# Planned attention and feed-forward kernel: first-pass sums held until a tile's last gate, gates ranked early, two kinds of copies moved to VectorE

## The chip, the cores and the metric

The kernel runs on one core of one Trainium2 chip. A core has five engines that run side by side, each with its own queue worked off in order: TensorE (PE, matrix products; its weight loads are shown as PEld), VectorE (DVE), ScalarE (ACT), GpSimd (POOL) and SyncE (SP, which only issues DMAs here). Data lies in DRAM, in SBUF (128 partitions) and in PSUM, which takes the products of TensorE and has eight banks of 128 x 512 float32. The metric is device time in microseconds: the median of several runs. Smaller is better.

## The reference

```
scores = 0.125 * q @ k.T            # 8 batches x 8 heads, 576 tokens, head size 64
scores = where(block_i >= block_j, scores, -1e9)      # blocks of 64 tokens
attn = softmax(scores) @ v
x = attn.transpose(0, 2, 1, 3).reshape(4608, 512)     # tokens x heads*size
h = x @ w_in                                          # 512 -> 2048
g = h * erf(softplus(h))
out = g @ w_out                                       # 2048 -> 512
```

Everything is float32. The kernel keeps float32 accuracy by splitting operands: each is written as a high part that TensorE takes exactly (fp32r, or fp16 for the probabilities) and a low part, the difference, and a product is made of three matmuls (high x high, high x low, low x high).

## The kernel before

**A plan.** The kernel does not issue its instructions as it builds them. Each step is put into a `Plan` with `add(engine, estimated ns, function, reads, writes)` and takes the priority `plan.prio` of that moment (a smaller number goes first). `Plan.order` then walks through estimated time, engine by engine: of the steps whose inputs are ready and whose buffers are free, the one with the smallest priority runs next. The order found there is the order in each engine's queue on the chip. `HOP` and `SPARE` are the extra time that it assumes between a step and one on another engine that needs it, the second for TensorE and for PSUM banks. Buffers of a tag in SBUF are given out in the order in which the steps were added; PSUM banks go to whoever asks first. A `token` is a buffer without memory that limits how many of something are under way.

**Attention** takes 64 heads, one for each `slot` n (0 to 63, with four more to run out). In slot n the plan adds: the load of head n+3 (`load_qk`: a DMA for `st` and one issued by GpSimd, two copies in SBUF by DMA, and the low parts on GpSimd, L456 and L457; four buffers `qks`); the maxima of head n+2 (`maxes`: scores `s` on TensorE L468, row maxima on VectorE L472 and L498, turned by TensorE and ScalarE and written by a small DMA `qk<-mt` into a row of q); the probabilities of head n (`probs`: scores `t`, L521 and L522; exp on ScalarE, L528, into `p32s`; the fp16 high part `ph` on ScalarE, L536, and the difference `pl` on VectorE, L537); for every second slot the products with v of a pair of heads (`pv`: `u`, L567, sums `us`, L593). Four heads are a quad; after each quad `normalise` makes reciprocals (L614), spreads them out (`rw`, L621, on ScalarE), turns them on TensorE (`rb`, L629), multiplies (`xs`, L632, VectorE), makes the high part (L634, ScalarE) and the low part (L635, GpSimd), and writes both to `x_d` in DRAM (L636). This is done once for each of the two pairs (`m(0)`, `m(1)`). The whole numbers of slots are the priorities; `PV` and the like shift some.

**First feed-forward pass.** Of 16 blocks of 128 hidden features the first `F1` = 6 are worked off for 18 tiles of `T` = 256 tokens, two blocks at a time: 3 `unit`s a tile, 54 in all. A unit (`moe_unit`) is: `up`, 24 matmuls into one PSUM bank `m_h` (L342); `gate`, a formula of one tanh (L314), four squares (L320) on ScalarE, two VectorE steps (L324, L328), then the high part `gh` (L329, ScalarE) and the low part `gl` (L330, GpSimd); `down`, 12 matmuls into two PSUM banks `o` (L363), one for each 128 tokens. A tile's `o` is summed over its three units; `store` copies it out (`ob`, L670) and writes it to `part_d`. A tile is known once its batch is normalised. The loop at the end of each slot adds units of known tiles:

```
at = max(n + BEHIND, 9 + BEHIND + (NT // T * NU - len(units1)) * spread)
if at - PACE > n and n < N + 3:
    break
unit1(at, False)
```

With `BEHIND` 1 and `PACE` 0, `at` is above n in every slot, so that units are added only in slot 67, with priority 68 or somewhat more and their gates at 65 (`GATE` -3). The last `TAIL` = 5 units have priorities of their own, from 70.

**Weights** are split by `load_weight` in two halves each: four or five VectorE steps (L287, L289, L292, L295, L297), two on ScalarE, two on GpSimd (L300, L301), with temporary buffers from the tags that gates and x use too. The six blocks of the first pass are added in the slots listed in `W1`, four of the second pass by `early_w2` after the last head, the others later.

**Second pass.** The other 10 blocks run over 9 tiles of 512 tokens; a unit is one block. The first tile also splits the weights that aren't there yet. At its end the sum of the first pass is added and written to the output. Some of its buffers (`w2`, `b`, `g`) exist only when all of attention is done.

Of the kernel before, what the change touches and what calls it, by code (L numbers as in the profile page):

```python
# [10 lines left out]
F16 = mybir.dt.float16  # L11
# [44 lines left out]
class Plan:  # L56
# [4 lines left out]
    SPARE = 500.0  # L61
    SWITCH = 90.0

# [4 lines left out]
    def add(self, eng, ns, fn, r=(), w=(), lag=0.0, mode="f", off=0.0):  # L68
        t = Task(len(self.tasks), eng, ns, lag, fn, self.prio + off, mode, self.era)
        for k in r:  # L70
            if k in self.written:
                t.deps.add(self.written[k])
            self.read.setdefault(k, []).append(t)
        for k in w:
            if k in self.written:
                t.deps.add(self.written[k])
            t.deps.update(self.read.pop(k, ()))
            self.written[k] = t
        t.deps.discard(t)
# [12 lines left out]
        self.tasks.append(t)  # L92
        return t
# [97 lines left out]
def tile_attention_moe(ctx: ExitStack, tc: tile.TileContext, qk, v, w, maskrows, sels, out):  # L191
# [21 lines left out]
    GATE = -3.0  # L213
# [90 lines left out]
    def gate(h, kh, n, name, gpool):  # L304
# [5 lines left out]
        bgh, bgl = (buf(gpool, [P, n], F32R, t, f"{name}_{t}") for t in ("gh", "gl"))  # L310
        br = [buf("m", [P, n], F32, t, f"{name}_{t}") for t in ("r0", "r1")]
        regs = [(br[0], br[0])]
        free = [((lambda: f32(bgl())), bgl), (br[1], br[1])]
        add("ACT", 690, lambda: nc.scalar.activation(br[0](), h(), AF.Tanh, bias=const(p1), scale=p0), r=kh, w=[br[0]])  # L314
        for k, (o, pp) in enumerate(zip(PROG, pars)):
            free += [regs[i] for i in sorted(set(o[1:])) if last[i] == k]
# [16 lines left out]
    def moe_unit(ws, xs, o, tw, nu, u, name, first, last, spread, oh, nh, gpool, at, rate, after=None):  # L333
# [19 lines left out]
        plan.prio = at + GATE  # L353
# [38 lines left out]
    p32s = [spool.tile([P, n], F32, name=f"p32_{i}") for i, n in enumerate(PN)]  # L392
    nc.gpsimd.memset(p32s[0][64:128, 768:], 0.0)
# [6 lines left out]
    ident16 = spool.tile([P, P], F16, name="id16")  # L400
    nc.vector.tensor_copy(ident16, ident)
# [108 lines left out]
    def probs(n, out):  # L510
# [4 lines left out]
        def one(j, q0, w_):  # L515
# [4 lines left out]
            def go():  # L520
# [7 lines left out]
            add("ACT", 160 + 0.84 * (w_ - skip), lambda: nc.scalar.activation(p32s[pt][:kk, c : c + w_ - skip], s()[:kk, skip:w_], AF.Exp, scale=SCALE),  # L528
                r=[s], w=[("p32", pt, j, q0)])

        def split(pt, keys):
            p = p32s[pt]
            ph = buf("a", [P, PN[pt]], F16, f"ph{pt}", f"ph{pt}_{n}", 4)
            pl = buf("a", [P, PN[pt]], F16, f"pl{pt}", f"pl{pt}_{n}", 4)
            keys = [("p32", pt, *k) for k in keys]
            add("ACT", 850, lambda: nc.scalar.copy(ph(), p), r=keys, w=[ph])  # L536
            add("DVE", 1250, lambda: nc.vector.tensor_tensor(out=pl(), in0=p, in1=ph(), op=ALU.subtract), r=keys + [ph], w=[pl])  # L537
            out.append((ph, pl))
# [62 lines left out]
    def normalise(b, qd, usbs, rs, krs):  # L601
# [14 lines left out]
        def m(pp):  # L616
            c = 2 * qd + pp
            xs = buf("a", [P, 2, S], F32R, "xs", f"xs_{nm}_{pp}")
            rw = buf("a", [P, 5, 2, D], F32, "rw", f"rw{nm}_{pp}", 1)
            for hf, k in enumerate((3, 2)):  # L620
                add("ACT", 510 - 110 * hf, lambda hf=hf, k=k: nc.scalar.copy(rw()[:, 3 * hf : 3 * hf + k], ri()[:, pp, :k, hf, :].unsqueeze(3).broadcast_to([P, k, 2, D])),  # L621
                    r=[ri], w=[(rw, hf)])
# [11 lines left out]
            add("ACT", 670, lambda: nc.scalar.copy(xs()[:, 0, :], f32(xs()[:, 1, :])), r=[(xs, 0), (xs, 1)], w=[(xs, 2)])  # L634
# [20 lines left out]
    os, hold = {}, {}  # L655
# [17 lines left out]
    def unit1(at, tail):  # L673
        t, u = units1.pop(0)
        plan.prio = at
        for s in (t, t + 1):
            if s in known and s not in x1:
                x1[s] = load_x("x", s * T, T)
        if u == 0:
# [3 lines left out]
                 hold[t], 3 if tail else NH, "g" if tail else "m", at, 0.05, marks.get(slot))  # L683
# [25 lines left out]
    def next_w1():  # L709
        plan.era = 0  # L710
        w1.append(room("w", len(w1)))
        load_weight(w1[-1], (("x", ("xh", "xl"), 2 * DM, 2), ("m", "r0", DM, 3), ("m", "r1", DM, 3)), len(w1) - 1)
# [11 lines left out]
    for slot in range(N + 4):  # L724
# [60 lines left out]
    def next_weight():  # L785
        if len(w2) < NF - F1:
            w2.append(room("w2" if len(w2) < NB + 2 else "w", F1 + len(w2)))
            load_weight(w2[-1], (("x", ("xh", "xl"), 2 * DM, 2), ("m", "gh", DM, 3), ("m", "gl", DM, 3)), F1 + len(w2) - 1)

    base = N + 6.0  # L790
# [88 lines left out]
```

## Time and profile before

| | us |
|---|---|
| median of 3 runs | 1395.18 |
| lowest, highest | 1393.9, 1398.31 |
| the profiled execution | 1394.03 |
| its span, first to last instruction | 1392.3 |

| engine | busy us | share of the span | instructions |
|---|---|---|---|
| TensorE | 1254.5 | 90% | 8168 |
| ScalarE | 973.5 | 70% | 1781 |
| VectorE | 804.2 | 58% | 1237 |
| GpSimd | 591.1 | 42% | 456 |

The profile comes from one execution, which has its own time. Busy times are shares of a span with stages of different limits, so the table alone doesn't say what bounds the kernel. The granted clock is the share of full speed that TensorE was given; its mean over the span is 0.922. In the views below an instruction is named by its source line (L320), its engine, and its output and input tiles; x576 is a count.

### The profile page before, as it was taken

How to read it: one execution, taken by the hardware profiler on the slowest of the kernel's cores; microseconds unless marked ns; L12 is line 12 of the kernel's file. 1: busy time of each engine (PE TensorE's matmuls, PEld its weight loads, DVE VectorE, ACT ScalarE, POOL GpSimd, SP SyncE). 2: the span in 40 equal slices, each digit the busy share in tenths (PEclk: the TensorE clock that was granted, in tenths of full speed). 3: DMA queues.
4: the chain of work that ended last, by engine and by line, in shares of the span. 5: the costliest groups of instructions: out<-in, count | busy, mean ns of one | idle time of the engine just before them, and what ended most of it. 6: DMA issues, size and time to landing. Idle time of an engine off the chain costs nothing.

```text
span 1392.3 us, 22070 instructions
## 1 busy us (share of the span) xinstructions
PE 1254.5 (90%) x8168; PEld 1038.4 (75%) x8168; DVE 804.2 (58%) x1237; ACT 973.5 (70%) x1781; POOL 591.1 (42%) x456
## 2 busy tenths in 40 slices
PE   7456688889998999999999998779999999999997
PEld 3345576677777778788989987568888888888885
DVE  4988867888777788886532218953333233333232
ACT  1445557788776787789877768557677676776764
POOL 5666545576564566654432225632222222222221
PEclk9756778899999999999999999889999999999999
DMA  9556376787767677753473223203203113113010
GB/s 238 150 139 161 94 201 170 185 209 204 190 181 176 169 199 207 179 158 124 154 255 105 91 76 137 76 2 120 99 23 122 61 61 121 61 61 121 1 61 31
DMA packets 89372, 179.97 MB, mean 129 GB/s; under 512 B 8540, under 2 KB 27292, under 8 KB 89264
## 3 DMA queue, kind: packets, MB, share of 16 engines
q1 hardware_dynamic: 79280, 159.41, 38.5%
q0 software_dynamic: 9344, 18.97, 6.5%
q8 instruction: 65, 1.06, 0.3%
q10 hardware_dynamic: 640, 0.17, 0.1%
q14 instruction: 43, 0.35, 0.1%
HBM read 112.29 MB, written 37.75 MB: 108 GB/s over the span
## 4 chain that ended last, share of the span: by engine, by line
PE 53%; DVE 5%; ACT 2%; issue 1%; DMA 1%; DVEq 0%; ACTq 0%
PE o L363 25%; PE m_h L342 24%; DVE bits L287 1%; DVE bits L289 1%; PE u L567 1%; DVE m_r L324 1%; DMA qk<-mt 1%; PE t L521 1%; ACT m_r L320 1%; PE t L522 1%; PE s L468 1%; DVE sq L292 0%; DVE pl L537 0%; DVE bits L295 0%; PE rt L611 0%
## 5 line engine op out<-in xcount | busy, mean ns | idle before, releaser
L320 ACT ACTIVATE m_r<-m_r,c 128x512 f32<-128x512 f32 x576 | 406.3, 720 | 88.1 <-DVE m_r L324 61.6
L330 POOL TENSOR_TENSOR m_gl<-m_r,m_gh 128x512 fp32r<-128x512 f32 x144 | 189.0, 1314 | 511.8 <-ACT m_gh L329 298.4
L324 DVE SCALAR_TENSOR_TENSOR m_r<-m_r,m_r 128x512 f32<-128x512 f32 x144 | 125.6, 873 | 289.7 <-ACT m_r L320 268.7
L342 PE MATMUL m_h<-xh,whi 128*128 128x256 f32 (+1 forms) x648 | 208.9, 322 | 0.1
L342 PE MATMUL m_h<-xl,whi 128*128 128x256 f32 (+1 forms) x648 | 207.4, 320 | 0.0
L342 PE MATMUL m_h<-xh,wlo 128*128 128x256 f32 (+1 forms) x648 | 207.3, 320 | 0.0
L472 DVE TENSOR_REDUCE mx<-s 64x1 f32<-64x288 f32 (+4 forms) x384 | 163.9, 464 | 61.2 <-PE s L468 60.5
L528 ACT ACTIVATE p<-t 128x288 f32<-128x288 f32 (+4 forms) x384 | 135.3, 386 | 74.1 <-PE t L522 32.6
L363 PE MATMUL o<-whi,m_gh 128*128 128x512 f32 x432 | 173.7, 402 | 14.6 <-ACT m_gh L329 14.3
L521 PE MATMUL t<-qk 69*128 69x288 f32 (+4 forms) x384 | 136.3, 359 | 45.0 <-DMA qk<-mt 15.5
L328 DVE SCALAR_TENSOR_TENSOR m_r<-m_r,m_h 128x512 f32<-128x512 f32 x144 | 98.7, 685 | 134.5 <-ACT m_r L320 134.5
L363 PE MATMUL o<-wlo,m_gh 128*128 128x512 f32 x432 | 172.6, 400 | 0.0
L537 DVE TENSOR_TENSOR pl<-p,ph 128x832 f16<-128x832 f32 (+1 forms) x128 | 151.6, 1186 | 28.9 <-ACT ph L536 28.6
L468 PE MATMUL s<-qk 68*128 68x256 f32 (+3 forms) x384 | 119.4, 372 | 42.6 <-DVE mx L472 24.9
L314 ACT ACTIVATE m_r<-m_h,c 128x512 f32<-128x512 f32 x144 | 98.5, 684 | 78.1 <-PE m_h L342 77.2
L456 POOL TENSOR_TENSOR qk<-st,qk 64x576 fp32r<-64x576 f32 x64 | 106.6, 1669 | 69.8 <-DMA qk<-qk 40.0
L457 POOL TENSOR_TENSOR qk<-st,qk 64x576 fp32r<-64x576 f32 x64 | 108.1, 1688 | 60.9 <-DMA qk<-qk 57.7
L342 PEld LDWEIGHTS m_h<-xh,whi 128*128 128x128 f32 x648 | 124.5, 192 | 10.9 <-DVE mx L472 0.4
L342 PEld LDWEIGHTS m_h<-xl,whi 128*128 128x128 f32 x648 | 124.5, 192 | 10.0
L342 PEld LDWEIGHTS m_h<-xh,wlo 128*128 128x128 f32 x648 | 124.3, 192 | 8.5
L522 PE MATMUL t<-qk 128*128 128x288 f32 (+4 forms) x384 | 126.2, 333 | 0.0
L363 PE MATMUL o<-whi,m_gl 128*128 128x512 f32 x432 | 126.1, 394 | 0.0
(83 smaller groups left out, 2357.9 us busy)
## 6 DMA issues: line engine op xcount, KB each, us to landing
st<-qk SPq DMA_DIRECT2D x64, 288.0 KB
qk<-qk POOLq DMA_DIRECT2D x64, 288.0 KB, 4.8
qk<-qk SPq DMA_DIRECT2D x64, 288.0 KB
x_d<-xs SPq DMA_DIRECT2D x32, 576.0 KB
raw<-w SPq DMA_DIRECT2D x32, 512.0 KB
v<-v SPq DMA_DIRECT2D x16, 640.0 KB
qk<-qk SPq DMA_DIRECT2D x64, 144.0 KB
xh<-x_d SPq DMA_DIRECT2D x18, 512.0 KB
```

The costliest lines, as they stand in the source:

```text
L320: add("ACT", 722, lambda r=r, a=a, pp=pp: nc.scalar.activation(r[0](), a[0](), AF.Square, bias=const(pp[1]), scale=pp[0]), r=[a[1]], w=[r[1]])
L324: add("DVE", 890, lambda r=r, a=a, c=c, pp=pp, ops=ops: nc.vector.scalar_tensor_tensor(out=r[0](), in0=a[0](), scalar=pp[0], in1=c[0](), o ...
L330: add("POOL", 1450, lambda: nc.gpsimd.tensor_tensor(out=bgl(), in0=g[0](), in1=f32(bgh()), op=ALU.subtract), r=[g[1], bgh], w=[bgl])
L342: nc.tensor.matmul(hk()[:, k, :], lhsT=a(0)[:, cc * P : (cc + 1) * P], rhs=x()[:, cc, :], start=cc == 0 and i == 0, stop=cc == NCC - 1 and ...
L363: nc.tensor.matmul(o[c](), lhsT=a()[:, sl], rhs=b_(1), start=first and k == 0 and not lo and b_ is whi, stop=last and k == nu - 1 and lo)
L457: add("POOL", 1780, lambda: nc.gpsimd.tensor_tensor(out=t[D:, 1, :], in0=st()[D:, :], in1=f32(t[D:, 1, :]), op=ALU.subtract), r=[st], w=Q( ...
L468: add("PE", mmns(w_), lambda: nc.tensor.matmul(s()[:r, c0 : c0 + w_], lhsT=qh[:K, i * P : i * P + r], rhs=kh[:K, k0 : k0 + w_], start=True ...
L472: add("DVE", 145 + 1.07 * w_, lambda: nc.vector.tensor_reduce(out=mx[:r, col : col + 1], in_=s()[:r, c0 : c0 + w_], axis=AX.X, op=ALU.max, ...
L521: nc.tensor.matmul(s()[:kk, :w_], lhsT=kh[:K, ks], rhs=qh[:K, q0 : q0 + w_], start=True, stop=False)
L522: nc.tensor.matmul(s()[:kk, :w_], lhsT=klh[:, ks], rhs=qhl[:, q0 : q0 + w_], start=False, stop=True)
L528: add("ACT", 160 + 0.84 * (w_ - skip), lambda: nc.scalar.activation(p32s[pt][:kk, c : c + w_ - skip], s()[:kk, skip:w_], AF.Exp, scale=SCALE),
L537: add("DVE", 1250, lambda: nc.vector.tensor_tensor(out=pl(), in0=p, in1=ph(), op=ALU.subtract), r=keys + [ph], w=[pl])
```

## The change

Times in the plan aside, the change does this:

- **Held sums.** For tiles below `HT` = 14 the down-projections of a tile are collected in `held` and added only after the tile's last gate, all for one `o` bank, then all for the other. Tiles 14 to 17 sum as before. The gate buffers are four (`NG`) where they were three, the two scratch buffers `r0`, `r1` two each (`NR`) where they were three. (The `gl` buffer is no longer listed as scratch; no gate ever took it as such.)
- **Early units.** Units are added as soon as their tile is known. Their matmuls have priorities from 1000 (`FILL`), behind all attention; their gates have `LEAD` + 1.1 x unit = 10 to 63, in among attention's slots. For the tail and the second pass `GATE` is -8 where it was -3.
- **Weights of the first pass**: four in slots 2, 4, 6, 8 and two when the first tile's third unit is added, with priority 13 at the earliest.
- **Copies.** `rw` (64) and the high part of `xs` (32) go from ScalarE to VectorE.
- **Buffers.** Two `p32` buffers of each kind where there was one; one `xs` and one `ob` where there were two; `ident16`, which only warms TensorE, is a view of `ident`.
- **The plan's own numbers.** `SPARE` 300 for 500, `PV` -1.2 for -0.7, and `DRAIN`: ScalarE and VectorE steps that read PSUM rank 0.7 of a slot earlier. The second difference `pl` is estimated at 1130 ns for 1250 and stays on VectorE.

```diff
-    SPARE = 500.0
+    SPARE = 300.0
...
+        if eng in ("ACT", "DVE") and any((k[0] if isinstance(k, tuple) else k).tag[1] == "PSUM" for k in r if isinstance(k[0] if isinstance(k, tuple) else k, Buf)):
+            t.prio += self.DRAIN
...
-    GATE = -3.0
+    GATE = -8.0
+    NG, NR = 4, 2
+    HT = 14
+    NP = (2, 2)
+    NX = 1
...
-        plan.prio = at + GATE
+        plan.prio = at + GATE if when is None else when
...
-        for a in sorted(((k, c, lo) for k in range(nu) for c in range(tw // P) for lo in (False, True)),
-                        key=lambda a: (a[2], a[0], a[1]) if spread else (a[1], a[2], a[0])):
+        steps = [(a[1], lambda a=a: down(*a)) for a in sorted(((k, c, lo) for k in range(nu) for c in range(tw // P) for lo in (False, True)),
+                                                           key=lambda a: (a[2], a[0], a[1]) if spread else (a[1], a[2], a[0]))]
+        if held is not None:
+            held.extend(steps)
+            if not last:
+                return
+            steps = sorted(held, key=lambda s: s[0])
+            held.clear()
+        for c, f in steps:
             plan.prio += rate
-            down(*a)
+            f()
...
-    p32s = [spool.tile([P, n], F32, name=f"p32_{i}") for i, n in enumerate(PN)]
+    p32s = [[spool.tile([P, n], F32, name=f"p32_{i}_{j}") for j in range(NP[i])] for i, n in enumerate(PN)]
...
-    ident16 = spool.tile([P, P], F16, name="id16")
-    nc.vector.tensor_copy(ident16, ident)
+    ident16 = ident.bitcast(F16)[:, :P]
...
-            add("DVE", 1250, lambda: nc.vector.tensor_tensor(out=pl(), in0=p, in1=ph(), op=ALU.subtract), r=keys + [ph], w=[pl])
+            eng, ns, on = (("DVE", 1250, nc.vector), ("DVE", 1130, nc.vector))[pt]
+            add(eng, ns, lambda: on.tensor_tensor(out=pl(), in0=p, in1=ph(), op=ALU.subtract), r=keys + [ph], w=[pl])
...
-            xs = buf("a", [P, 2, S], F32R, "xs", f"xs_{nm}_{pp}")
+            xs = buf("a", [P, 2, S], F32R, "xs", f"xs_{nm}_{pp}", NX)
...
-                add("ACT", 510 - 110 * hf, lambda hf=hf, k=k: nc.scalar.copy(rw()[:, 3 * hf : 3 * hf + k], ri()[:, pp, :k, hf, :].unsqueeze(3).broadcast_to([P, k, 2, D])),
+                add("DVE", 430 - 100 * hf, lambda hf=hf, k=k: nc.vector.tensor_copy(rw()[:, 3 * hf : 3 * hf + k], ri()[:, pp, :k, hf, :].unsqueeze(3).broadcast_to([P, k, 2, D])),
...
-            add("ACT", 670, lambda: nc.scalar.copy(xs()[:, 0, :], f32(xs()[:, 1, :])), r=[(xs, 0), (xs, 1)], w=[(xs, 2)])
+            add("DVE", 450, lambda: nc.vector.tensor_copy(xs()[:, 0, :], f32(xs()[:, 1, :])), r=[(xs, 0), (xs, 1)], w=[(xs, 2)])
...
-    W1 = [1, 2, 3, 4, 7, 8]
+    W1 = [2, 4, 6, 8]
...
-    PACE = 0.0
+    FILL = 1000.0
+    LEAD, GRADE = 10.0, 1.1
...
-    PV = -0.7
+    PV = -1.2
...
-            ob = buf("m", [P, DM], F32, "ob", f"ob{t}_{c}", 2)
+            ob = buf("m", [P, DM], F32, "ob", f"ob{t}_{c}", 1)
...
-            if s in known and s not in x1:
+            if s in known and s not in x1 and (s == t or len(w1) == F1):
...
         moe_unit(w1, x1[t], os[t], T, 2, u, f"m1_{t}_{u}", u == 0, u == NU - 1, not tail,
-                 hold[t], 3 if tail else NH, "g" if tail else "m", at, 0.05, marks.get(slot))
+                 hold[t], 3 if tail or t >= HT else NH, "g" if tail else "m", at, 0.05, None, held if t < HT else None, None if tail else LEAD + (t * NU + u) * GRADE)
...
-            at = max(n + BEHIND, 9 + BEHIND + (NT // T * NU - len(units1)) * spread)
-            if at - PACE > n and n < N + 3:
-                break
-            unit1(at, False)
+            t, u = units1[0]
+            while len(w1) < 2 * u + 2:
+                plan.prio = n + 2 * u
+                next_w1()
+                plan.era = 0
+            unit1(FILL + NT // T * NU - len(units1), False)
...
-    base = N + 6.0
+    base = 2.0 * FILL
```

More of the change, by code (lines that the diff above doesn't have):

```diff
@@ L309, in gate @@
                 last[i] = k
[L310 to L313, printed above, removed]
+        bgh, bgl = (buf(gpool, [P, n], F32R, t, f"{name}_{t}", NG if gpool == "m" else None) for t in ("gh", "gl"))
+        br = [buf("m", [P, n], F32, t, f"{name}_{t}", NR) for t in ("r0", "r1")]
+        regs, free = [(br[0], br[0])], [(br[1], br[1])]
         add("ACT", 690, lambda: nc.scalar.activation(br[0](), h(), AF.Tanh, bias=const(p1), scale=p0), r=kh, w=[br[0]])
         for k, (o, pp) in enumerate(zip(PROG, pars)):
-            free += [regs[i] for i in sorted(set(o[1:])) if last[i] == k]
+            over = [regs[i] for i in sorted(set(o[1:])) if last[i] == k]
+            free += over
             r = free.pop()
@@ L331, in gate, with moe_unit @@
         return bgh, bgl
-    def moe_unit(ws, xs, o, tw, nu, u, name, first, last, spread, oh, nh, gpool, at, rate, after=None):
+    def moe_unit(ws, xs, o, tw, nu, u, name, first, last, spread, oh, nh, gpool, at, rate, after=None, held=None, when=None):
         bh = bank(f"{name}_h")
@@ L654, in tile_attention_moe @@
     units1 = [(t, u) for t in range(NT // T) for u in range(NU)]
-    os, hold = {}, {}
+    os, hold, held = {}, {}, []
     TAIL = 5
```

18 lines of the change are left out of this document (10 added, 8 removed).

## The prediction

> **What bounds the kernel now.** I read the windows view first, cut where the work changes: attention to 645 us, the rest of the first feed-forward pass to 841, a hand-over to 950, the second pass to the end. Columns are busy us (and instructions) of PE, weight loads, VectorE (DVE), ScalarE (ACT) and GpSimd (POOL), then the granted TensorE clock, DMA share and GB/s.
>
> ```profile
> core 0: us, PE busy (x) PEld busy (x) DVE busy (x) ACT busy (x) POOL busy (x), PEclk, DMA share, GB/s
> 35.00:180.00 145.00, 87.47 (x655) 69.49 (x654) 128.28 (x188) 76.11 (x164) 87.47 (x63) 0.68 0.54 139
> 180.00:350.00 170.00, 151.53 (x1405) 123.95 (x1403) 136.08 (x243) 127.25 (x281) 98.17 (x71) 0.86 0.76 194
> 350.00:500.00 150.00, 134.97 (x1173) 109.28 (x1173) 114.86 (x200) 110.41 (x241) 84.70 (x64) 0.90 0.70 178
> 500.00:645.00 145.00, 138.46 (x1329) 117.00 (x1328) 116.63 (x200) 118.60 (x259) 79.76 (x59) 0.96 0.63 172
> 645.00:841.00 196.00, 195.49 (x1251) 178.04 (x1250) 68.68 (x96) 152.09 (x242) 62.09 (x47) 1.00 0.41 141
> 841.00:950.00 109.00, 85.45 (x353) 68.68 (x352) 84.25 (x89) 71.09 (x115) 57.76 (x39) 0.89 0.23 78
> 950.00:1392.00 442.00, 433.72 (x1904) 357.95 (x1902) 140.46 (x194) 310.90 (x474) 103.46 (x80) 0.99 0.20 70
> ...
> 592.00:627.00 35.00, 33.50 (x347) 28.81 (x346) 27.79 (x46) 30.36 (x70) 17.65 (x13) 1.00 0.54 163
> 180.00:645.00 465.00, 424.96 (x3904) 350.23 (x3903) 367.57 (x640) 356.26 (x779) 262.62 (x193) 0.91 0.70 182
> ```
>
> From 645 to 841 and from 950 on TensorE is simply full at full clock: only less PE work shortens these. Before 645 it isn't. From 180 to 645, busy time times clock is 424.96 x 0.91 = 387 us of 465, or 0.83. VectorE is the busiest of the others: 495.85 us in the 610 from 35 to 645 (four rows added), 0.813, and 0.885 in the first 145 us.
>
> Next, how much feed-forward work lies on each side of 645: the grouped view, first from 180 to 645 (three lines), then from 645 to 841.
>
> ```profile
> L342 PE MATMUL m_h<-xh,whi 128*128 128x256 f32 x144 | 43.3, 301 | 0.1
> L324 DVE SCALAR_TENSOR_TENSOR m_r<-m_r,m_r 128x512 f32<-128x512 f32 x17 | 16.4, 963 | 0.5 <-ACT usb L572 0.4 <-ACT m_r L320 0.2
> L472 DVE TENSOR_REDUCE mx<-s 64x1 f32<-64x288 f32 (+4 forms) x298 | 127.8, 466 | 46.9 <-PE s L468 46.1
> ...
> L342 PE MATMUL m_h<-xh,wlo 128*128 128x256 f32 x277 | 78.4, 283 | 0.0
> ```
>
> A unit has 2 x 4 such matmuls. So 144/8 = 18 of the 54 first-pass units go up during attention and 277/8 = 34.6 behind it, at 196/34.6 = **5.66 us a unit**, up and down together. Why only 18? The view of single lines gives the first start of each step:
>
> ```profile
> L342 PE MATMUL m_h<-xh,whi x648: 274/283/628, 197.2 to 1375.2; 128*128 128x256 f32 x108, 128*128 128x512 f32 x54
> L314 ACT ACTIVATE m_r<-m_h,c x144: 667/689/698, 201.8 to 1376.1; 128x512 f32<-128x512 f32 x144
> L329 ACT CAST m_gh<-m_r x144: 601/611/630, 248.1 to 1381.8; 128x512 fp32r<-128x512 f32 x144
> L363 PE MATMUL o<-whi,m_gh x432: 387/389/797, 381.2 to 1384.7; 128*128 128x512 f32 x144
> ```
>
> The first gate takes from 201.8 to 248.1 for about 5 us of work, and the first down-projection comes at 381.2. Gates have the plan's priority 65, behind all attention (at is n+1 or more in every slot, so the loop breaks until slot 67). The down-projections rank last and need two PSUM banks for three units. With three gate buffers, everything then stands.
>
> **The change part by part.** Prices:
>
> ```profile
> L320 ACT ACTIVATE m_r<-m_r,c 128x512 f32<-128x512 f32 x576 | 406.3, 720 | 88.1 <-DVE m_r L324 61.6
> L324 DVE SCALAR_TENSOR_TENSOR m_r<-m_r,m_r 128x512 f32<-128x512 f32 x144 | 125.6, 873 | 289.7 <-ACT m_r L320 268.7
> L328 DVE SCALAR_TENSOR_TENSOR m_r<-m_r,m_h 128x512 f32<-128x512 f32 x144 | 98.7, 685 | 134.5 <-ACT m_r L320 134.5
> L621 ACT COPY rw<-ri 128x384 f32<-128x384 f32 x64 | 26.3, 454 | 9.0 <-PE rb L629 8.5 <-DVE ri L614 0.5
> L634 ACT CAST xs<-xs 128x576 fp32r<-128x576 f32 x32 | 21.3, 666 | 1.4 <-POOL xs L635 1.0 <-DVE xs L632 0.2
> ...
> L295 DVE TENSOR_SCALAR bits<-sq x32: 414/427/1511, 39.3 to 915.5; 128x512 int32<-128x512 int32 x32
> L287 DVE TENSOR_SCALAR bits<-raw x32: 406/650/1521, 34.5 to 911.5; 128x512 int32<-128x512 int32 x32
> L632 DVE TENSOR_TENSOR xs<-usb,rb x64: 334/444/556, 109.7 to 643.9; 128x384 f32<-128x384 f32 x32, 128x192 f32<-128x192 f32 x32
> ```
>
> 1. Copies to VectorE. ScalarE loses 26.3 + 21.3 = 47.6 us. VectorE gains 64 copies of 384 or 256 columns and 32 of 576. No row shows them; the nearest are L295 (one input, 512 columns, least 0.414) and L632 (334 to 556 ns). I take 0.40 and 0.45 us: 64 x 0.40 + 32 x 0.45 = **40 us**, all in attention. Upper end: L287, of L295's size, has a median 0.24 above its least, and the longest of both is 1.1 above; with 0.53 more for each of 96 copies it is 91.
>
> 2. Gates early, sums held. Gate i now has priority 10 + 1.1 i in slots, in among attention. Held steps run bank by bank, 18 matmuls each, so one bank serves where two stood through three units, and the down-projections of a tile come before the next tile's ups. Each unit moved ahead of the end of attention takes 5.66 us from the full PE stage and adds 0.873 + 0.685 = 1.56 us to VectorE there (ScalarE: 0.69 + 4 x 0.72 + 0.61 = 4.2).
>
> 3. How many units move. Two limits. Data: batch b is complete in slot 9 + 8b, so by slot 65 the plan can know 15 tiles, 45 units. PE: room for about 21 more by part 4's check. A mean over 500 us won't hold its best window, so I take 16 more, **34 units**.
>
> 4. The sum. VectorE then has 495.9 + 40 + 16 x 1.56 = 561 us to do from 35 us to the end of attention. At what share? 0.813 was the mean, 0.885 where split weights stood ready to fill each gap; the 46.9 us before L472 are such gaps, and gates now fill them. I take 0.86: 652 us, so attention ends at 687, **+42**. Behind it 16 x 5.66 = **-91** us. Net **-49**. PE check: 387 + 91 = 478 us of full-clock work in 687 - 167 = 520 (the start from part 5) is 0.92; the 592 to 627 row, the best of attention, shows 0.957. So 16 fit, 21 just do (506 of 529), 24 don't (523 of 535).
>
> 5. Weights. Six were split in slots 1 to 8, now four, and two in about slot 13. The rows from 35 to 180:
>
> ```profile
> L289 DVE SCALAR_TENSOR_TENSOR bits<-raw,bits 128x512 int32<-128x512 int32 x12 | 14.7, 1222 | 0.4
> L292 DVE SCALAR_TENSOR_TENSOR sq<-sq,bits 128x512 f32<-128x512 f32 x12 | 13.3, 1112 | 0.6
> L297 DVE SCALAR_TENSOR_TENSOR bits<-raw,bits 128x512 f32<-128x512 uint32 x12 | 10.5, 872 | 0.4
> L287 DVE TENSOR_SCALAR bits<-raw 128x512 int32<-128x512 int32 x11 | 9.0, 817 | 0.0
> L295 DVE TENSOR_SCALAR bits<-sq 128x512 int32<-128x512 int32 x12 | 7.1, 595 | 0.4
> ```
>
> 54.6/12 = 4.55 us a half, so four halves, 18 us, leave the crowded start and come back later: nothing in the sum, but the first unit starts 18 - 5 (eight short and four long copies) = 13 us sooner, near 184, and the PE window of part 4 opens at 167. If slot 13 isn't filled by other work, the 13 us are the price.
>
> 6. Buffers and order. These waits bear on the rest:
>
> ```profile
> ACT p L528 <- DVE pl L537: 17.6, 7, 3.7
> DVE xs L632 <- POOL xs L635: 4.3, 2, 2.6
> PE o L363 <- ACT m_gh L329: 23.6, 6, 6.6
> ...
> qk<-qk POOLq DMA_DIRECT2D x64, 288.0 KB, 4.8
> L635 POOL TENSOR_TENSOR xs<-xs 128x576 fp32r<-128x576 f32 x32 | 46.9, 1472 | 26.3 <-ACT xs L634 19.3 <-issue 6.3 <-DMA qk<-qk 0.3
> ```
>
> Doubled p32 takes away the 17.6 us of ScalarE waits; ScalarE isn't the bound (432 - 48 + 67 = 451 of 652), so this counts only inside the 0.86. One xs buffer adds a wait: the second product of a quad waits for the first's copy, subtraction (1.47) and write; a 288 KB transfer lands in 4.8 us, and this is 576 KB, so 7 to 12 us, 16 times. Behind it on VectorE stand the next maxima and differences, and for them PE's next scores. The plan puts other work between: 0 to 16 x 4 = 64 us, taken at 0, as the two waits of 4.3 us in all suggest, and as the plan's order allows for the write. One ob buffer makes ScalarE wait likewise, hidden by its 30% idle time; uncovered, some 4.8 us (the 288 KB row) for each of 18 second halves, 86, if nothing else stood between them. DRAIN, SPARE and PV only sort; gates at -8 run ahead of the weights' splitting in the hand-over, whose 23.6 us are PE waiting for gates behind it: -10 to +10, taken at 0. The first four late weights (8 halves, 36 us of VectorE) and 20 gates (31 us) hide in the remaining 20 x 5.66 = 113 us; with under 12 units left they would show. ident16, the free list and the 1130 entry change no work beside one 0.2 us cast; pl stays on VectorE.
>
> **The rivals.** (a) *More fits in.* Short matmuls count as busy for 283 to 301 ns where back-to-back ones of this size follow each other by less (36 matmuls of a unit in 5.66 us, 157 ns), so PE's 0.83 may be partly empty. At share 0.885 with 42 units (24 more): (495.9 + 40 + 37)/0.885 = 647, +37, less 24 x 5.66 = 136: -99, about 1296. Against it: 523 us of PE work in 515.
>
> (b) *VectorE sets attention's pace and few units move* (slower). TensorE's fillers still rank behind all attention for a PSUM bank. With the share left at 0.813 and 8 more units: (40 + 12.5)/0.813 = +65, less 45: +19, 1414. It decides below the point where (40 + 1.56 x)/0.813 = 5.66 x, 13 units.
>
> (c) *The copies and GpSimd hold each other up* (slower). L287 and L295 at three times their least show VectorE held by something while GpSimd works. At 0.53 more for each copy VectorE has 51 us more, 51/0.86 = 59: -49 + 59 = +10, 1405. The Trainium skill, "SBUF — State Buffer", section "SBUF: two separate sides", says that a two-port VectorE operation and GpSimd take an exclusive lock on a shared port pair, and that an fp32 SBUF-to-SBUF copy is such an operation, which also keeps descriptors of GpSimd-issued DMAs from being written. The rows of L287 agree as to the stretch; none shows the copies or the descriptors.
>
> (d) *It cancels*: between (b) and the forecast, about 11 to 14 units, 1395.
>
> **How the numbers follow.** The profiled execution took 1394.0 us for a span of 1392.3; -49 gives 1345, and the median of the runs lies 1.2 above it: **1346**. Chances: forecast 0.57 (1320 to 1375), (a) 0.20, (d) 0.05, (b) 0.12, (c) 0.06. About 0.3%, 4 us, is what can be told from no change. Faster 0.57 + 0.20 = 0.77, same 0.05, slower 0.18. The range takes in most of (a) and the near side of (c): 1290 to 1402.
>
> **What would show it.** Right: L363 starts before 300, not at 381; near 34 x 8 matmuls of L342's first kind lie before the last L521; attention ends near 687 with VectorE at 0.86 or more; the full PE stage behind it is about 113 us; 950 to the end is unchanged. Part 1 is wrong if L621 and L634 on VectorE average above 0.5 us. Wrong altogether: fewer than 31 units before the end of attention, VectorE still near 0.81, or new waits at L632 on the write of xs.

## The result, and the profile after

The changed kernel takes 1411.05 us (median of 4, 1408.68 to 1416.51) against 1394.54: a ratio of **1.012, interval 1.0083 to 1.0157**. It is slower by 1.2%, where 1346 was forecast. The profiled execution took 1409.69 us for a span of 1407.5, 15.2 longer than before.

The windows view cut at the same events, the last product with the reciprocals (L632 before, L647 after), a point of the second pass with the same work left, and the end. First the kernel before, then the changed one.

```profile
35.00:643.90 608.90, 511.33 (x4549) 418.66 (x4548) 494.75 (x825) 431.35 (x941) 350.10 (x255) 0.85 0.66 171
643.90:950.00 306.10, 282.04 (x1610) 247.78 (x1609) 154.03 (x188) 224.20 (x357) 119.85 (x85) 0.96 0.35 119
950.00:1392.30 442.30, 433.72 (x1904) 357.95 (x1902) 140.46 (x194) 310.90 (x474) 103.46 (x80) 0.99 0.20 70
```

```profile
core 0: us, PE busy (x) PEld busy (x) DVE busy (x) ACT busy (x) POOL busy (x), PEclk, DMA share, GB/s
35.00:717.80 682.80, 594.70 (x4951) 493.19 (x4952) 546.87 (x950) 443.64 (x930) 369.85 (x266) 0.85 0.61 162
717.80:965.00 247.20, 220.16 (x1215) 189.03 (x1214) 135.07 (x165) 172.97 (x275) 106.96 (x75) 0.95 0.36 122
965.00:1407.00 442.00, 434.45 (x1905) 358.79 (x1903) 140.02 (x196) 313.08 (x476) 103.36 (x80) 0.99 0.20 70
```

The ledger is short: attention is 73.9 us longer, the stretch behind it 58.9 shorter, the second pass the same. Sum +15. VectorE's share in attention is 546.87/682.8 = 0.80, not 0.86; the clock there is 0.85 as before. How many units moved, and how the early ones went, is in the grouped view up to 718 us and in the views of single lines:

```profile
L349 PE MATMUL m_h<-xh,whi 128*128 128x256 f32 x224 | 68.2, 304 | 1.7 <-DVE mx L486 1.7
```

```profile
L320 ACT ACTIVATE m_r<-m_h,c x144: 663/690/698, 179.6 to 1391.3; 128x512 f32<-128x512 f32 x144
L336 ACT CAST m_gh<-m_r x144: 601/608/642, 186.5 to 1396.6; 128x512 fp32r<-128x512 f32 x144
L370 PE MATMUL o<-whi,m_gh x432: 387/389/797, 248.2 to 1400.0; 128*128 128x512 f32 x144
```

The first gate now takes 7 us, where it took 46, and the first down-projection comes at 248, not 381. So the change does what it says. But 224/8 = 28 units are up by the end of attention, 10 more than before and not 16; at 5.66 us that is 58 us to be saved behind it, and the ledger shows 58.9, against 74 paid ahead. The copies, in the grouped view by shape:

```profile
L636 DVE COPY rw<-ri 128x256 f32<-128x256 f32 x32 | 23.7, 739 | 0.0
L649 DVE CAST xs<-xs 128x576 fp32r<-128x576 f32 x32 | 18.6, 580 | 0.9
L636 DVE COPY rw<-ri 128x384 f32<-128x384 f32 x32 | 17.3, 540 | 0.0
```

The smaller shape has the longer mean, so something besides size stretches them (the least of L636 is 0.277 us). Together they are 59.6 us, or 56.5 in attention with overlaps counted once, not 40.

Attention's own waits changed in kind. Lines of the waits view from 180 to 645 us (total, times, longest), before and then changed:

```profile
ACT p L528 <- PE t L522: 24.3, 34, 2.8
ACT m_r L314 <- PE m_h L342: 2.7, 3, 1.4
DVE m_r L328 <- ACT m_r L320: 0.8, 2, 0.6
DVE mx L472 <- PE s L468: 46.1, 40, 4.9
DVE pl L537 <- ACT ph L536: 21.0, 30, 2.5
```

```profile
ACT p L542 <- PE t L536: 69.1, 62, 5.2
ACT m_r L320 <- PE m_h L349: 16.8, 15, 4.7
DVE m_r L331 <- ACT m_r L327: 15.5, 13, 4.8
DVE m_r L335 <- ACT m_r L327: 5.2, 4, 1.5
DVE mx L486 <- PE s L482: 27.0, 27, 4.6
DVE pl L552 <- ACT ph L550: 2.2, 7, 0.6
```

Some waits grew, from 28 us in all to 107: ScalarE waits for the score tiles `t` and for the sums of units, VectorE for the gates' squares. Others shrank, from 67 to 29: VectorE's on the score tiles `s` and on the high parts. Over all lines of this stretch ScalarE's waits went from 105 to 152 us and VectorE's from 94 to 84. As fillers, gates were hardly waited for by anyone in a queue; in among attention they are.

One loss stands out in ScalarE's timeline behind attention, and in TensorE's waits from 780 to 830 us:

```profile
797.48 1.48 ACT L327 ACTIVATE m_r<-m_r,c 128x512 f32<-128x512 f32 x2
811.01 0.58 ACT L686 COPY ob<-o 128x512 f32<-128x512 f32 x1 [12.06 <-DMA part_d<-ob]
```

```profile
PE o L370 <- ACT m_gh L336: 12.2, 2, 11.8
```

With one `ob` buffer the second store of a tile waits for the write of the first, here 12 us, and the gate behind it in ScalarE's queue makes TensorE stand for 11.8.

### The profile page after: what moved, and what is told of

It is laid out like the page before. It is cut to its first block, busy times and chain, and to the rows that moved or that the text cites. A ratio compares the mean times of both kernels' runs of the same rounds, so it can differ in the third digit from the quotient of the medians.

```text
span 1407.5 us, 21929 instructions
## 1 busy us (share of the span) xinstructions
PE 1277.5 (91%) x8168; PEld 1053.7 (75%) x8168; DVE 839.1 (60%) x1332; ACT 933.4 (66%) x1685; POOL 600.2 (43%) x457
## 4 chain that ended last, share of the span: by engine, by line
PE 65%; DVE 14%; ACT 8%; DMA 5%; issue 3%; POOL 1%; SPq 0%; ACTq 0%; DVEq 0%; POOLq 0%
PE o L370 24%; PE m_h L349 24%; ACT m_r L327 4%; PE u L582 4%; PE t L535 3%; DMA qk<-mt 3%; PE t L536 3%; PE s L482 3%; DVE pl L552 3%; DVE mx L486 2%; DVE sq L299 2%; PE us L608 1%; PE rt L626 1%; DVE m_r L331 1%; DVE bits L296 1%
## 5 line engine op out<-in xcount | busy, mean ns | idle before, releaser
L337 POOL TENSOR_TENSOR m_gl<-m_r,m_gh 128x512 fp32r<-128x512 f32 x144 | 195.9, 1360 | 487.5 <-ACT m_gh L336 389.2
L331 DVE SCALAR_TENSOR_TENSOR m_r<-m_r,m_r 128x512 f32<-128x512 f32 x144 | 122.0, 847 | 306.9 <-ACT m_r L327 267.0
L349 PE MATMUL m_h<-xh,whi 128*128 128x256 f32 (+1 forms) x648 | 211.5, 326 | 1.8 <-DVE mx L486 1.7
L349 PE MATMUL m_h<-xl,whi 128*128 128x256 f32 (+1 forms) x648 | 209.3, 323 | 0.0
L349 PE MATMUL m_h<-xh,wlo 128*128 128x256 f32 (+1 forms) x648 | 209.0, 322 | 0.0
L370 PE MATMUL o<-whi,m_gh 128*128 128x512 f32 x432 | 178.3, 413 | 26.2 <-ACT m_gh L336 25.0
L542 ACT ACTIVATE p<-t 128x288 f32<-128x288 f32 (+4 forms) x384 | 132.2, 387 | 98.0 <-PE t L536 93.9
L535 PE MATMUL t<-qk 69*128 69x288 f32 (+4 forms) x384 | 135.8, 363 | 36.9 <-DMA qk<-mt 18.6
L482 PE MATMUL s<-qk 68*128 68x256 f32 (+3 forms) x384 | 113.3, 397 | 37.7 <-DMA qk<-qk 18.1
L349 PEld LDWEIGHTS m_h<-xh,whi 128*128 128x128 f32 x648 | 126.7, 196 | 13.9 <-issue 2.1
L349 PEld LDWEIGHTS m_h<-xl,whi 128*128 128x128 f32 x648 | 126.4, 195 | 10.6
L349 PEld LDWEIGHTS m_h<-xh,wlo 128*128 128x128 f32 x648 | 126.0, 194 | 8.6
L370 PE MATMUL o<-whi,m_gl 128*128 128x512 f32 x432 | 131.3, 404 | 0.2 <-POOL m_gl L337 0.2
```

Source lines behind the costliest of these rows:

```text
L331: add("DVE", 890, lambda r=r, a=a, c=c, pp=pp, ops=ops: nc.vector.scalar_tensor_tensor(out=r[0](), in0=a[0](), scalar=pp[0], in1=c[0](), o ...
L337: add("POOL", 1450, lambda: nc.gpsimd.tensor_tensor(out=bgl(), in0=g[0](), in1=f32(bgh()), op=ALU.subtract), r=[g[1], bgh], w=[bgl])
L349: nc.tensor.matmul(hk()[:, k, :], lhsT=a(0)[:, cc * P : (cc + 1) * P], rhs=x()[:, cc, :], start=cc == 0 and i == 0, stop=cc == NCC - 1 and ...
L370: nc.tensor.matmul(o[c](), lhsT=a()[:, sl], rhs=b_(1), start=first and k == 0 and not lo and b_ is whi, stop=last and k == nu - 1 and lo)
L482: add("PE", mmns(w_), lambda: nc.tensor.matmul(s()[:r, c0 : c0 + w_], lhsT=qh[:K, i * P : i * P + r], rhs=kh[:K, k0 : k0 + w_], start=True ...
L535: nc.tensor.matmul(s()[:kk, :w_], lhsT=kh[:K, ks], rhs=qh[:K, q0 : q0 + w_], start=True, stop=False)
```

## The experiments

Two readings were open. *Pace*: VectorE sets the length of attention, at a fixed share of its time, so the 56 us of copies cost some 70. *Waits*: no engine sets it alone, and the order of the queues does. The runs come from several chips, each with runs of the kernel before beside them, so differences are taken from the ratios; 0.001 is 1.4 us.

**Copies back; second pl to GpSimd; copies alone; two ob buffers.** The edits (e4 also takes back the second `p32` buffer of one kind):

```diff
 e1, on the changed kernel (e3 is the reverse, on the kernel before)
-                add("DVE", 430 - 100 * hf, lambda hf=hf, k=k: nc.vector.tensor_copy(rw()[:, ...
+                add("ACT", 510 - 110 * hf, lambda hf=hf, k=k: nc.scalar.copy(rw()[:, ...
-            add("DVE", 450, lambda: nc.vector.tensor_copy(xs()[:, 0, :], ...
+            add("ACT", 670, lambda: nc.scalar.copy(xs()[:, 0, :], ...
 e2, on the changed kernel
-            eng, ns, on = (("DVE", 1250, nc.vector), ("DVE", 1130, nc.vector))[pt]
+            eng, ns, on = (("DVE", 1250, nc.vector), ("POOL", 1800, nc.gpsimd))[pt]
 e4, on the changed kernel
-    NP = (2, 2)
+    NP = (2, 1)
-            ob = buf("m", [P, DM], F32, "ob", f"ob{t}_{c}", 1)
+            ob = buf("m", [P, DM], F32, "ob", f"ob{t}_{c}", 2)
```

> The changed kernel with the 96 copies (rw, high part of xs) back on ScalarE; all else as changed. Theory 'pace': the length of attention is VectorE's work over a fixed share of 0.80 (547 us in 683 measured). The copies measured 38.7 + 17.8 = 56.5 us, so attention shortens by about 56.5/0.80 = 70 us, to about 650; some 3 to 4 fewer units fit into the shorter time (28 in 540 us), which cost 20 us behind it: 1411 - 50 = 1361. Rival 'waits': VectorE has 20% of slack and attention is set by the order of the queues and the waits between engines; then the result is within 15 us of 1411.

> The changed kernel with the second difference pl (64 of 768 columns, 69.5 us on VectorE before) moved to GpSimd, estimated at 1800 ns in the plan. 'Pace': VectorE loses 69.5 us, attention shortens by 87, some 4 units fewer fit: about 1411 - 64 = 1347. 'Waits': within 15 us of 1411, or slower, since GpSimd gets about 64 x 1.5 to 1.8 = 96 to 115 us more ahead of the splits of q and k.

> The kernel before with only the 96 copies moved to VectorE. 'Pace': VectorE gains 56.5 us, at its share of 0.81 attention grows by 70, some 3 more filler units fit in: 1394 + 70 - 15 = about 1449. 'Waits': VectorE's idle time takes the copies, ScalarE is eased by 47.6 us: within 15 us of 1394.

> The changed kernel with two ob buffers again; for room in SBUF the second kind of p32 has one buffer as before. The trace of the changed kernel has one ScalarE wait of 12.1 us at 799 us for the write of ob, and TensorE stands 11.8 us behind it. If this is a loss of its own, it goes: 1411 - 12 to 14 = about 1398, with p32 giving back 0 to 5. Rival: the store is only one of many waits and the order settles elsewhere: within 5 us of 1411.

| run | us | ratio to before (interval) | attention ends at | units up by then |
|---|---|---|---|---|
| before | 1394.5 | 1 | 643.9 | 17.8 |
| changed | 1411.1 | 1.012 (1.0083 to 1.0157) | 717.8 | 28.0 |
| e1 copies on ScalarE | 1402.0 | 1.0075 (1.0044 to 1.0107) | 706.2 | 26.9 |
| e2 second pl on GpSimd | 1384.1 | 0.994 (0.9909 to 0.9971) | 707.7 | 30.0 |
| e3 before, with the copies | 1415.8 | 1.0172 (1.0104 to 1.0239) | 649.7 | 15.9 |
| e4 two ob | 1402.5 | 1.0076 (1.0046 to 1.0106) | 708.9 | 25.0 |

(Units are the first kind of up matmul of L342 or L349 before the last product with the reciprocals, over 8.) The windows of attention in e1, e3 and e16 (the copies on ScalarE and the second difference on GpSimd, listed further on):

```profile
35.00:706.20 671.20, 585.37 (x4896) 478.32 (x4895) 498.22 (x852) 470.22 (x1008) 367.65 (x263) 0.84 0.61 164
```

```profile
35.00:649.70 614.70, 517.22 (x4473) 415.78 (x4471) 540.06 (x920) 388.79 (x832) 342.77 (x252) 0.83 0.63 169
35.00:708.40 673.40, 584.01 (x4997) 484.33 (x4998) 473.92 (x798) 482.47 (x1029) 474.44 (x330) 0.87 0.61 167
```

*Pace*, a bound at a fixed share of VectorE's time, falls. With the copies gone VectorE is busy 498.22 of 671.2, 0.74, and attention is 12 us shorter instead of 70. In e16 the share goes down to 473.92/673.4 = 0.70, and attention is 9 us shorter than in the changed kernel. With the copies added to the kernel before, the share goes up to 540.06/614.7 = 0.88, attention grows by 6, and two fewer units fit in. A share that runs from 0.70 to 0.88, with attention's end moving by 12 us at most in either kernel, is not a bound.

That doesn't make VectorE's work free. e1 and e3 move copies between VectorE and ScalarE, so they show the price on one engine less the price on the other, and no run priced VectorE's work alone. e1 is 6 us faster than the changed kernel, which the next runs show to be within chance. e3 is 21 us slower than the mean of three orders of the kernel before (1.002, below) and slower than each of them, so there the copies seem to cost more on VectorE than on ScalarE. e4 brought 6 us, and no wait of ScalarE on the write of ob was left in it; see e8 for what 6 us mean here. e2 came out 25 us faster than the changed kernel, between its two forecasts; e17 and e18 test it again.

**TensorE's room, the gates' priority, and another order.**

```diff
 e5, on the kernel before (e6, on the changed one, leaves out the second matmul of each score tile, with the low parts of q and k)
+                nc.tensor.matmul(s()[:kk, :w_], lhsT=kh[:K, ks], rhs=qh[:K, q0 : q0 + w_], start=True, stop=True)
                 nc.tensor.matmul(s()[:kk, :w_], lhsT=kh[:K, ks], rhs=qh[:K, q0 : q0 + w_], start=True, stop=False)
 e7, on e1
-    LEAD, GRADE = 10.0, 1.1
+    LEAD, GRADE = 65.0, 0.0
 e8, on the changed kernel
-    HOP = 200.0
+    HOP = 210.0
```

> The kernel before with the first matmul of each score tile t (L521) issued twice, the second overwriting the first: 384 matmuls, 1856 columns a head, 0.82 us a head at the plan's price, 53 us more TensorE work in attention at full clock and nothing else; the plan knows of it. Theory 'full': TensorE, busy 0.91 of the time there at a clock of 0.91, has no room to give, so attention grows by 53/0.91 = 58 us, the filler units per time stay, and the time is about 1394 + 50 to 58 = 1448. Rival 'room' (the prediction's reading, 0.83 used of 0.957): the gaps take it, less than 15 us.

> The changed kernel without the second matmul of each score tile (L536, the products with the low parts of q and k, left out of the scores): 53 us less TensorE work in attention, waits and all other engines' work unchanged. 'Full': attention, which ended at 718, shortens by 53/0.89 = 60 us, the time is about 1411 - 55 = 1356. 'Room' or a bound by VectorE or by the chain from one head to the next: less than 15 us.

> The changed kernel with the copies on ScalarE (as e1, 1402, attention to 706) and all first-pass gates at priority 65, as before the change, instead of 10 to 63; held sums, buffers, weights' slots and the plan's numbers as changed. 'Full': each unit done during attention costs attention about 6.5 us and saves 5.66 behind it, so with the units back near 18 attention ends near 650 and the time is about 1402 - 8 = 1394. Rival: the buffers and the plan's numbers lengthen attention; then it stays near 700, and the units that are missing come behind it, 1402 + 40 = about 1440.

> The changed kernel with HOP 210 for 200 in the plan: no instruction is added or removed, only the order found by the plan shifts. It shows how much of any difference is the order's chance. All theories: 1411; within 5 us if single stalls like the 12 us one at 799 us don't matter, up to 15 us if they do.

| run | us | ratio to before (interval) | attention ends at | units up by then |
|---|---|---|---|---|
| e5 before, 53 us more TensorE work | 1406.4 | 1.0089 (1.0049 to 1.0128) | 657.4 | 18.6 |
| e6 changed, 53 us less | 1371.8 | 0.9846 (0.9804 to 0.9889) | 700.7 | 30.9 |
| e7 copies on ScalarE, gates late | 1411.4 | 1.0121 (1.0072 to 1.017) | 657.6 | 16.1 |
| e8 changed, HOP 210 | 1390.0 | 0.9981 (0.9952 to 1.001) | 712.5 | 27.8 |

e8 is the one that matters most. It has the same instructions as the changed kernel; only a constant of the plan differs, by 10 ns, which shuffles the order. It takes 1390 us, as much as the kernel before. So some 20 us, more than the whole result, can come from the order's chance.

"Full" falls with e5. The window of attention in e5:

```profile
35.00:657.40 622.40, 550.54 (x4940) 468.65 (x4938) 500.86 (x834) 439.03 (x946) 349.19 (x257) 0.88 0.65 170
```

TensorE was busy 39 us more in the window and its mean clock rose from 0.85 to 0.88; the busy time times clock went from 435 to 484, so about all of the 53 us were done in a window 13.5 us longer. The forecast was right that TensorE has room in attention. Its work isn't free there, though: e6, with 53 us less, is 0.027 below the changed kernel and 0.018, 25 us, below the mean of that kernel's four orders (1.003, below), between the 15 us of "room" and the 55 of "full".

e7 against e1 (gates late or early, all else alike) is the cleanest price of a moved unit: 10.8 units, 48.6 us of attention, **4.5 us each**, against 5.66 saved. The early gates gain 0.0046, 6 us, in time, which is within the chance of the order. With everything else of the change in place, e7's attention ends at 658 us, so the buffers and the plan's numbers alone don't lengthen it much.

**How far chance goes.** The same shift on both kernels:

> The kernel before with HOP 190 for 200: the same instructions in another order. Theory 'chance of the order': the two kernels are families of orders that overlap, spread some 10 to 20 us each, with means under 10 apart; then this lies anywhere from 1380 to 1415. Rival 'the change costs': the kernel before stays within 5 us of 1394 under such a shift, and the changed one was lucky once, at 1390.

> The kernel before with HOP 210. 'Chance': anywhere from 1380 to 1415; 'the change costs': 1394, within 5.

> The changed kernel with HOP 190. 'Chance': anywhere from 1385 to 1415, so that the mean of the changed kernel's orders comes near that of the other's; 'the change costs': 1405 to 1415.

> The changed kernel with HOP 220. 'Chance': anywhere from 1385 to 1415; 'the change costs': 1405 to 1415.

| run | us | ratio to before (interval) | attention ends at | units up by then |
|---|---|---|---|---|
| e9 before, HOP 190 | 1389.1 | 0.9983 (0.995 to 1.0015) | 654.4 | 21.0 |
| e10 before, HOP 210 | 1405.2 | 1.0081 (1.0048 to 1.0114) | 663.3 | 19.0 |
| e11 changed, HOP 190 | 1384.3 | 0.9931 (0.9885 to 0.9977) | 732.2 | 31.4 |
| e12 changed, HOP 220 | 1404.6 | 1.0077 (1.0047 to 1.0107) | 705.3 | 27.5 |

The two families overlap. The three orders of the kernel before have a mean ratio of 1.002, the four of the changed one 1.003 (from 0.993 to 1.012). The change as such is worth nothing that seven orders can tell; the order that it came with is the slowest of its four. What is the same in every order is the exchange: attention ends at 654 us on average with 19.25 units, or at 717 with 28.7. That is 63 us for 9.4 units, 6.7 us each with everything else that the change does. Behind attention the changed orders are 62 us shorter on average, 6.6 us a unit, so the exchange comes out even; what is saved there beyond 5.66 a unit was not traced.

Where an order loses time, it shows in the granted clock. A run's time multiplied by the mean clock of the same execution comes to 1274 to 1289 us (means of each run) for every run with the same TensorE work but one, while the times go from 1384 to 1425; the one is e13, below, at 1259. Single executions of one order go the same way: the nine of e11 run from 1372.95 us at 0.928 to 1393.07 at 0.913. e5, which only adds TensorE work, had a higher clock than the kernel before beside it, 0.935 for 0.92, and a product of 1313; e6 had 0.905 and 1242. So in these runs the clock goes with how full TensorE is kept. Whether a low clock or the gaps come first was not separated.

**What a unit costs attention.** ScalarE's 4.2 us a unit and the PSUM banks that a unit holds had not been priced yet.

```diff
 e13, on the changed kernel
+                if not (name.startswith("m1_") and k in (2, 4)):
                     add("ACT", 722, lambda r=r, a=a, pp=pp: nc.scalar.activation(r[0](), a[0](), AF.Square, ...
 e14, on the kernel before
+            if pt == 1:
+                add("ACT", 850, lambda: nc.scalar.copy(ph(), p), r=keys, w=[ph])
 e15, on the kernel before
-             "ps": ctx.enter_context(tc.tile_pool(name="ps", bufs=8, space=PSUM))}
+             "ps": ctx.enter_context(tc.tile_pool(name="ps", bufs=7, space=PSUM))}
```

(e13 leaves two steps out of the gate's formula and so computes another function. e15 has 7 in the plan's own count as well. e16 is e1 and e2 together.)

> The changed kernel without two of the four squares of each first-pass gate (left out of the formula): 54 x 2 x 0.72 us less ScalarE work, of which some 28 x 1.44 = 40 us in attention and the rest behind it, where TensorE sets the time. Theory 'ScalarE': a unit's price in attention is its ScalarE work (4.2 of 6.7 us); attention falls from 717 (mean of four orders) to about 675, the time by about 35 from 1397 (their mean) to 1362. Rival 'banks' or 'no one engine': attention within 15 us of 717, the time within 15 of 1397.

> The kernel before with the high part ph of the second kind copied twice on ScalarE (64 x 0.83 = 53 us, nothing else). 'ScalarE': attention grows from 654 (mean of three orders) by 45 to 55, the time from 1396 to about 1445. 'No one engine' or 'banks': as with TensorE's 53 us in e5, attention grows by less than 20, the time by less than 15.

> The kernel before with seven PSUM banks for eight. 'Banks': the early units' price is the one to three banks that their sums hold; then a bank less lengthens attention by 25 us or more (to 680 or above) or leaves clearly fewer units in it (under 15), and the time is 1415 or more. 'ScalarE' or 'no one engine': attention within 15 us of 654, units 16 to 21.

> The changed kernel with both moves: the second pl on GpSimd (e2, 1384) and the copies back on ScalarE (e1, 1402, against 1397 as the mean of four orders). If VectorE's work still tells, about 1375 to 1380; if e2's gain is a chance of the order, near 1397; if ScalarE is the limit once VectorE is eased, above e2, near 1395.

| run | us | ratio to before (interval) | attention ends at | units up by then |
|---|---|---|---|---|
| e13 changed, two squares fewer | 1353.3 | 0.9702 (0.9639 to 0.9765) | 700.2 | 30.9 |
| e14 before, 53 us more ScalarE work | 1425.2 | 1.0244 (1.0202 to 1.0286) | 675.6 | 19.0 |
| e15 before, seven banks | 1425.1 | 1.0245 (1.0206 to 1.0283) | 666.8 | 17.0 |
| e16 second pl on GpSimd, copies on ScalarE | 1389.0 | 0.9983 (0.9957 to 1.0008) | 708.4 | 29.6 |

e13 to e15 lie outside the families, as e3 and e6 do. The windows of attention in e13, e14 and e15:

```profile
35.00:700.20 665.20, 595.61 (x5056) 498.06 (x5056) 557.62 (x961) 416.70 (x886) 382.71 (x269) 0.87 0.63 170
```

```profile
35.00:675.60 640.60, 544.82 (x4586) 441.48 (x4585) 506.13 (x840) 488.77 (x1019) 354.27 (x257) 0.82 0.63 167
```

```profile
35.00:666.80 631.80, 537.04 (x4503) 435.16 (x4503) 499.39 (x828) 431.46 (x936) 333.85 (x254) 0.81 0.62 165
```

53 us more on ScalarE cost 22 us of attention at the same number of units and 1.0244 - 1.002 = 0.022, some 31 us, of time. Fifty-three more on TensorE had cost 0.007, about 9. Two squares fewer in each gate, about 43 us of ScalarE in attention (30 gates at 1.44), gave 16 us of attention and two units more, some 29 us in all at 5.66 a unit. The time fell by 0.033, 45 us, but that also holds what the 23 gates behind attention save. Yet ScalarE is busy only 0.65 to 0.71 of attention in both kernels; in e14 it is 488.77/640.6 = 0.76. Neither expectation is met in full: attention moved less than "ScalarE" said and more than "no one engine". A bank less cost about 31 us of time too, as the banks' rival had it, but attention grew by 13 us, not 25, and two fewer units fit in. So ScalarE's work and the banks both have a price, and neither is the whole. Each of these runs is one order, and orders of one kernel lay 0.010 and 0.019 apart, so the prices may be off by 10 us and more.

Neither e13 nor e14 changes ScalarE's load alone. The gates of e13 are also two steps shorter, and the second copy of e14 stands between an exp and its difference. In e14 VectorE waited 17.9 us for high parts from 180 to 640 us, against 21.0 before, so the longer chain didn't show there; that speaks for the queue and doesn't settle it.

From e5, e6, e13 and e14 a unit's 4.2 us of ScalarE at 0.58 to 0.67 (31 of 53, 29 of 43) and its 5.66 us of TensorE at 0.2 to 0.5 come to an estimate of 3.6 to 5.6 us. That holds the 4.5 of e7. The 6.7 of the families, which have the rest of the change in them, lies above it; a unit's 1.56 us of VectorE and the banks are not in the estimate, and in the changed kernel the banks were not tried apart.

e16 at 0.9983 is 6 us below the mean of the changed orders and inside their spread. It lies between its three forecasts and chooses none of them.

**Is there a version that beats both?** e2 was the fastest that leaves nothing out, beside e11.

> e2 (second difference pl on GpSimd) with HOP 190. If the move is a gain of its own, its orders lie 10 or more below the mean of the changed kernel's orders (1397): 1378 to 1388. If e2 was a lucky order: 1390 to 1410.

> e2 with HOP 210. As for e17: 1378 to 1388 for a gain of its own, 1390 to 1410 for a lucky order.

e17 took 1397.95 us (ratio 1.0027, 0.9996 to 1.0058), e18 1390.0 (0.9962, 0.9916 to 1.0007). Their attention ends at 705.5 and 698.6 us, with 29.5 and 27 units. With e2 the mean ratio of three orders is 0.998, 0.5% below the changed kernel's 1.003, inside the spread of either. Both fell on the side of luck, e18 at its edge. e11 and e2 are orders faster than the kernel before by 0.6 to 0.7%; no edit among these is a gain of its own that could be shown.

## Why the prediction was wrong

**What bounds the kernel** held: the second pass didn't move, a unit behind attention is worth 5.66 us or a little more (58.9 us for 10.25 of them), and TensorE has room in attention (e5).

**Part 1** was mis-sized: the copies took 56 us in place of 40, inside the bounds of 40 to 91; they average 0.64 (L636) and 0.58 (L649), above the 0.5 named as the sign. Against ScalarE doing them, they cost 6 us in the changed kernel, within chance (e1), and 21 in the one before (e3).

**Part 3** was mis-sized too: 10 units came, not 16. So 58.9 us were saved behind attention, not 91: 32 of the 64 us between the forecast (-49) and the result (+15).

**Part 4 is the step that failed**, and it makes the other 32: attention grew by 74 us, not 42. The step turned VectorE's work into a length of attention by a share that the gates were to raise from 0.81 to 0.86, since they would fill gaps. The share was 0.80, as the prediction's own sign of being wrong had it. And the share isn't a mechanism: e1, e16 and e3 move it to 0.74, 0.70 and 0.88 without moving attention's end by more than 12 us. TensorE was the only other engine weighed, for its room. ScalarE was set aside as "451 of 652", with 30% idle, and the PSUM banks had no term. e14 shows that ScalarE's work costs 0.4 to 0.6 of its length (22 us of attention, 31 of time, for 53), though ScalarE idles for a third of attention; e15 shows a price for a bank, and e6 one for TensorE's work. VectorE's own price stays open.

How a gate lengthens attention is argued and not shown alone: ranked among attention's slots, it stands in ScalarE's in-order queue ahead of exps and copies that release PSUM banks and feed the differences, and it may itself wait there for its sums (16.8 us on L349); as a filler at priority 65 it came late because it came where little waited.

**Part 5** was right in its sign and low in size: the first unit's first matmul came at 174.7 (197.2 before), where 184 was forecast. **Part 6**: the xs buffer's wait is small (1.5 us of VectorE on the write in all), but the cover of the ob buffer was not there once: 12 us behind attention, where the text had said 4.8. Its cost was counted as nothing.

**The rivals.** (b) gave 1414 with a share of 0.81 and 8 more units; the run had 0.80, 10 and 1411. Its number was right by luck: VectorE's pace, its reason, is not borne out, and other orders of the same kernel took 1384 to 1405. Its second half, that few units move, was right. (c) showed in the copies' stretch, by 16 us and not 51, and didn't decide; its 0.53 us a copy stands in no row, 0.17 came, and in the rows shown L287 and L295 average 2.0 and 1.4 times their least, not three. (a) is refuted by the 28 units and the length of attention, not by TensorE's room. What no case of mine allowed for is that a reshuffled plan moves the time by 20 us by chance: the range of each case should have been wider by that, and the case "it cancels", given 0.05, is what the mean of the families shows. That 1411 lies outside the stated 1290 to 1402 is partly this chance, since the mean of the four orders, about 1398, would lie inside; but no order gained what the forecast said, and on average attention grew by 63 us, not 42, for 9.4 units, not 16.

## What to carry to other kernels

In a kernel whose order comes from a planner, run each version with two or three harmless shifts of the plan before a difference of 1% is put down to an edit. An engine's idle share says nothing of whether more work on it is free: add a known amount of work to each engine in turn and see what it costs. Moving work from one engine to another only shows the difference of two prices. And work ranked in among other work is paid for: here a unit moved ahead so cost 4.5 us of attention (e7) of the 5.66 that it saved.

## What the runs showed of the hardware

Moving 64 of the differences, 66 us of work, from VectorE to GpSimd (e2) didn't lighten VectorE. Over the whole execution, with all its other work the same, it is busy 839.1 us in the changed kernel and 838.1 in e2; in e17 and e18 it is 846.8 and 836.6. Only with the copies on ScalarE did some of it come off, 26 us: 794.8 in e1, 768.6 in e16. A step of one column shows it best; the view of the line in the changed kernel, then in e2 (least, median, longest ns):

```profile
L512 DVE TENSOR_TENSOR mx<-mx x64: 137/146/1787, 23.9 to 667.0; 64x1 f32<-64x1 f32 x64
```

```profile
L512 DVE TENSOR_TENSOR mx<-mx x64: 138/524/5594, 23.3 to 653.6; 64x1 f32<-64x1 f32 x64
```

It has no work to speak of, so 524 ns is mostly standing, and it stands longer where GpSimd is busier (478 us for 364 up to 707.7 us). This line alone takes back 24 us, 49.4 for 25.5. The Trainium skill, "SBUF — State Buffer", section "SBUF: two separate sides", says that a VectorE operation with two SBUF inputs and a GpSimd operation that reads SBUF lock each other out for a whole instruction; these rows agree. The longest, 5.6 us, would by estimate be several GpSimd instructions in a row, since a difference takes 1.8 us there.
